# Moving the splitting of pass-2 weights and gated values from GpSimd to VectorE and ScalarE

## The chip, the cores and the metric

The kernel runs on one core of a Trainium2 chip. The metric is the device time of one execution, in microseconds (us). Five engines work in parallel, each with its own queue of instructions which it takes strictly in order: TensorE (PE in the profile, its weight loads PEld), VectorE (DVE), ScalarE (ACT), GpSimd (POOL) and SyncE (SP, which here issues the DMAs). An instruction that waits for a semaphore holds up all that stand behind it on the same engine.

## The reference

```
x = causal attention of 4 x 8 heads, 576 tokens, head size 64   -> x [2304, 512]
h = x @ w_in                       # w_in  [512, 2048]
g = h * clip(h + 3, 0, 6) / 6      # the gate
x2 = g @ w_out                     # w_out [2048, 512]
m = max(x2 @ w1, x2 @ w2, x2 @ w3) # each [512, 768]
out = m @ w_out2                   # [768, 512]
```

All inputs are float32 to the caller; the weights reach the chip as 64-bit floating-point words of the same values, so each weight tile is first decoded from integer bits to float32.

## The kernel before, in words

Nearly every matrix product is done as three matmuls on a split operand pair (`three`, L427): both factors are held as a high half (the value rounded to the matmul's float32r format) and a low half (the value minus its high half), and high x high, high x low and low x high are added up in one PSUM bank. So every operand has to be split once: one rounding copy (`rounded`, L326) and one subtraction (`minus`, L344) with two inputs in SBUF.

The work has four stages: attention (until about 345 us in the trace), the first hidden layer (`hidden1`, `gate`, `reduce1`), the second one (`hidden2`, products with combined weights and inputs) and the last product (`reduce2`). The first hidden layer runs in two passes. Pass 1 (z = 0) takes the first 6 of 16 blocks of 128 hidden channels, for all 8 units of 288 tokens, and lies partly under the attention. Pass 2 (z = 1) takes the other 10 blocks for all 8 units. For each unit and block PE makes 12 matmuls into a PSUM bank (tile ps_h); then `gate` runs four steps: ACT writes `u` (L955), DVE writes `g` (L959) and with that frees the PSUM bank, ACT rounds `g` into the high half of `gt` (L331, called gh here), and a subtraction writes the low half (L346, called gl). PE then uses `gt` for 12 matmuls of `reduce1` (tile ps_x), which go between those of later gates.

The 20 late weight blocks (10 of w_in, 10 of w_out) are decoded when attention is over, between about 366 and 463 us: a 512 KB DMA into `raw` (two buffers), a square on ACT (L385), four DVE instructions on 128x512 (L387, L393, L398, L403), and then the two halves of `w`: the rounding (L333, called wh) and the subtraction (L346, called wl). Six more blocks, of w_out2 (keys "o2"), go through the same code later. The `raw` buffer is free after L403, so the next load is issued then.

Which engine does a splitting step is looked up in the table `ON` (L226). Where an entry names two engines, the one that is free first in a planner takes it: the whole kernel is written by small threads which a simulated clock (`Flow`, L108) advances with assumed costs (`COST`, L316), and the instructions of each engine are put into the program in the order in which the planner dispatches them. So an entry in `ON` sets not only where an instruction runs but can also move later ones, on all engines.

Of the kernel before, what the change touches and what calls it, by code (L numbers as in the profile page):

```python
# [9 lines left out]
F32 = mybir.dt.float32  # L10
# [18 lines left out]
U1 = S // 2  # L29
# [3 lines left out]
NA = 6  # L33
# [170 lines left out]
def dve2(n):  # L204
    return 0.068 + n * 0.00104
# [6 lines left out]
def act2(n):  # L212
    return 0.051 + n / 1200.0
# [6 lines left out]
def pool2(n):  # L220
# [3 lines left out]
DMA = ("SP", 0.45)  # L224
POOL, ACT, DVE = ("POOL",), ("ACT",), ("DVE",)
ON = {  # L226
    "wh": DVE,
    "wl": POOL,
    ("qb", "h", True): ACT,
    ("qb", "h", False): POOL + ACT,  # L230
    ("qb", "l", True): POOL + DVE,
# [14 lines left out]
    "xh": ACT + DVE,  # L246
    "xl": POOL,
    "gh": ACT,
    "gl": POOL + DVE,
    "part": ACT,  # L250
}

# [2 lines left out]
def attn_moe_moe2(ctx, tc, q, k, v, s, w_in, w_out, w1, w2, w3, w_out2, out):  # L255
# [40 lines left out]
    def make(item, shape, dtype, name):  # L296
        pl, tag = item
        if pl is None:
            return views[tag]
        return pl.tile(shape, dtype, tag=tag, name=name, bufs=1)  # L300
# [10 lines left out]
    def round_to(dst, src):  # L311
        pool.tensor_scalar(
            out=dst, in0=src, scalar1=1.0, scalar2=1.0, op0=ALU.mult, op1=ALU.mult
        )
# [11 lines left out]
    def rounded(dst, src, n, engines):  # L326
        e = yield [(x, COST["copy"][x](n)) for x in engines]
        if e == "POOL":
            round_to(dst, src)
        elif e == "ACT":  # L330
            act.activation(dst, src, AF.Copy)  # L331
        else:
            vec.tensor_copy(dst, src)  # L333
# [10 lines left out]
    def minus(dst, a, b_, n, engines):  # L344
        e = yield [(x, COST["sub"][x](n)) for x in engines]
        (pool if e == "POOL" else vec).tensor_tensor(  # L346
            out=dst, in0=a, in1=b_, op=ALU.subtract
        )
# [21 lines left out]
    def weight(key):  # L370
        return ready.setdefault(key, event())

    def bits_in(src, out):
        r = yield RAW.get()
        raw = make(r, [P, 512], I64, "raw")
        yield DMA
        copy(raw, src)
        yield flow.landing(8 * P * 512)
        am = yield AM.get()
        m = make(am[1], [P, 512], F32, "dm")  # L380
        a = make(am[0], [P, 512], U32, "da") if out is None else out.bitcast(U32)
        bits = raw.bitcast(U32).rearrange("p (n t) -> p n t", t=2)
        lo, hi = bits[:, :, 0], bits[:, :, 1]
        yield "ACT", act1(512)
        act.activation(m, hi.bitcast(F32), AF.Square)  # L385
        yield "DVE", dve2(512)
        vec.scalar_tensor_tensor(  # L387
            out=m, in0=m, scalar=LEAST * LEAST, in1=hi.bitcast(F32),
            op0=ALU.is_ge, op1=ALU.mult,
        )  # L390
        top = m.bitcast(U32)
        yield "DVE", dve1(512)
        vec.tensor_scalar(  # L393
            out=a, in0=top, scalar1=3, scalar2=0x3FFFFFF8,
            op0=ALU.logical_shift_left, op1=ALU.bitwise_and,
        )
        yield "DVE", dve2(512)
        vec.scalar_tensor_tensor(  # L398
            out=a, in0=top, scalar=0xC0000000, in1=a,
            op0=ALU.bitwise_and, op1=ALU.bitwise_or,  # L400
        )
        yield "DVE", dve2(512)
        vec.scalar_tensor_tensor(  # L403
            out=a, in0=lo, scalar=29, in1=a,
            op0=ALU.logical_shift_right, op1=ALU.bitwise_or,
        )
        RAW.put(r)
        if out is not None:
            AM.put(am)
        return a.bitcast(F32), am  # L410

    def decode(src, store, key):
        item = yield store.get()
        wf, am = yield from bits_in(src, None)
        dst = make(item, [P, 2, 512], F32R, "w")
        yield from rounded(dst[:, 0, :], wf, 512, ON["wh"])
        yield from minus(dst[:, 1, :], wf, dst[:, 0, :].bitcast(F32), 512, ON["wl"])
        AM.put(am)
        weight(key).set((dst, item))

# [509 lines left out]
    def hidden1():  # L930
        for z in range(2):
            for u in range(NU):
                x, xi = yield x_ready[z, u]
                for f in range(z * NA, NA if z == 0 else NF):
                    w, wi = yield weight(("i", f))
                    gi = yield GT.get()
                    bank = yield M.get()
                    ps = make(bank, [P, U1], F32, "ps_h")
                    for kk in range(KD):
                        yield "PE", 3 * mm(U1), kk < KD - 1  # L940
                        three(
                            ps, w_slice(w, kk), (x[:, 0, kk, :], x[:, 1, kk, :]),
                            kk == 0, kk == KD - 1,
                        )
                    flow.start(flow.cur.prio, gate(z, u, f, ps, bank, gi))
                    if u == NU - 1:
                        (W if z == 0 else W2).put(wi)
                X.put(xi)
        x_over.set()

    def gate(z, u, f, ps, bank, gi):
        ui = yield UU.get()
        ut = make(ui, [P, U1], F32, "u")
        yield "ACT", act2(U1) + 0.093
        act.activation(ut, ps, AF.Relu, bias=half, scale=1.0 / 6.0)  # L955
        g2 = yield GG.get()
        g = make(g2, [P, U1], F32, "g")
        yield "DVE", dve2(U1)
        vec.scalar_tensor_tensor(  # L959
            out=g, in0=ut, scalar=1.0, in1=ps, op0=ALU.min, op1=ALU.mult  # L960
        )
        M.put(bank)
        UU.put(ui)
        t = make(gi, [P, 2, U1], F32R, "gt")
        yield from rounded(t[:, 0, :], g, U1, ON["gh"])
        yield from minus(t[:, 1, :], g, t[:, 0, :].bitcast(F32), U1, ON["gl"])
        GG.put(g2)
        gt_ready[z, u, f].set((t, gi))

# [100 lines left out]
    def out_weight(j):  # L1070
        yield from decode(w_out2[j], W, ("o2", j))
        w, item = weight(("o2", j)).value
        ev = yield from load(o2_d[j], w, 8 * P * 512)
        yield ev
        W.put(item)
        o2_stored[j].set()
# [307 lines left out]
    def main():  # L1384
# [15 lines left out]
        for f in range(NB):  # L1400
            flow.start(NS + f, decode(w_in[NA + f], W2, ("i", NA + f)))
        for f in range(NB):
            flow.start(NS + AFTER + f, decode(w_out[NA + f], W2, ("o", NA + f)))
# [130 lines left out]
```

## Time and profile before

| | |
|---|---|
| time, median of 3 runs | 982.18 us (979.78 to 984.79) |
| the profiled execution | 978.72 us |
| its span, first to last instruction | 976.9 us |
| PE busy | 931.7 us (95%) |
| PE weight loads busy | 870.5 us (89%) |
| VectorE busy | 701.5 us (72%) |
| ScalarE busy | 451.7 us (46%) |
| GpSimd busy | 390.0 us (40%) |

An engine's busy time says how long its instructions were running, waits for a shared resource inside an instruction included. The shares are averages over stages; rows of single stretches follow below. A matmul of 288 columns shows about 0.29 us, but consecutive ones start about 0.13 us apart.

### The profile page before, as it was taken

Reading aid. Unit: us, or ns where it says so; the run is one execution under the profiler, and the core shown is the slowest. Engines: PE = TensorE matmul, PEld = TensorE weight load, DVE = VectorE, ACT = ScalarE, POOL = GpSimd, SP = SyncE. Lnnn points to the kernel's source line nnn. Section 1 sums busy time; section 2 is a strip of 40 time slices with the busy share of each in tenths; the row PEclk is TensorE's granted clock in tenths of the full one; section 3 lists DMA queues with packets and bytes.
Section 4 is the critical chain, followed back from the end, with each engine's and each line's share of the span. In section 5 each row is a group of like instructions: output and inputs, shape, how many; then the busy total and the mean of one; then the engine's idle time right before and its main releaser. Section 6 shows DMA issues by size and latency. Waiting matters only on the chain.

```text
span 976.9 us, 19063 instructions
## 1 busy us (share of the span) xinstructions
PE 931.7 (95%) x6532; PEld 870.5 (89%) x6532; DVE 701.5 (72%) x1819; ACT 451.7 (46%) x1146; POOL 390.0 (40%) x430
## 2 busy tenths in 40 slices
PE   9988799999899999899999999999899999999998
PEld 5555589888889999899999999998899999999998
DVE  5899899878898729999548777449987676666300
ACT  3566488676776734343433334334433232333321
POOL 5578668555665324444324332226731000011000
PEclk7789799999999999999999999999899999999999
DMA  5689778695785345554545646401312120255522
GB/s 173 177 225 275 206 184 221 168 256 161 182 229 140 118 136 167 185 184 149 170 157 176 227 148 214 141 18 32 86 51 73 38 85 31 94 182 147 160 78 74
DMA packets 87482, 144.56 MB, mean 148 GB/s; under 512 B 9532, under 2 KB 58684, under 8 KB 87384
## 3 DMA queue, kind: packets, MB, share of 16 engines
q1 hardware_dynamic: 87384, 143.33, 50.4%
q8 instruction: 52, 0.85, 0.4%
q14 instruction: 46, 0.38, 0.1%
HBM read 82.79 MB, written 33.96 MB: 120 GB/s over the span
## 4 chain that ended last, share of the span: by engine, by line
PE 66%; DVE 14%; DMA 9%; issue 5%; POOL 2%; ACT 2%; SPq 2%; DVEq 0%; POOLq 0%; ACTq 0%
PE ps_j L430 6%; PE ps_j L431 6%; PE ps_j L429 6%; PE ps_s L762 6%; PE ps_x L429 4%; PE ps_h L429 4%; PE ps_h L430 4%; PE ps_x L431 4%; PE ps_h L431 4%; PE ps_x L430 4%; PE pt L826 3%; DMA kt<-kb 3%; PE px L867 3%; PE ps_o L430 3%; PE ps_o L431 3%
## 5 line engine op out<-in xcount | busy, mean ns | idle before, releaser
L429 PE MATMUL ps_x<-gt,w 128*128 128x288 f32 x512 | 153.8, 300 | 6.1 <-DVE g L959 5.5
L346 POOL TENSOR_TENSOR gt<-g,gt 128x288 fp32r<-128x288 f32 x100 | 87.8, 878 | 179.3 <-ACT gt L331 169.0
L429 PE MATMUL ps_h<-x,w 128*128 128x288 f32 x512 | 153.9, 301 | 0.3 <-DVE g L959 0.3
L431 PE MATMUL ps_x<-gt,w 128*128 128x288 f32 x512 | 152.2, 297 | 1.4 <-POOL w L346 1.4
L430 PE MATMUL ps_h<-x,w 128*128 128x288 f32 x512 | 151.7, 296 | 0.0
L430 PE MATMUL ps_x<-gt,w 128*128 128x288 f32 x512 | 151.3, 295 | 0.0
L431 PE MATMUL ps_h<-x,w 128*128 128x288 f32 x512 | 151.1, 295 | 0.0
L340 POOL TENSOR_SCALAR e<-e,tiny 128x256 f32<-128x256 f32 (+4 forms) x152 | 106.4, 706 | 92.2 <-DVE tiny L791 47.3
L430 PE MATMUL ps_j<-xf,wf 128*128 128x288 f32 x432 | 129.5, 300 | 3.1 <-POOL xf L346 2.7
L429 PE MATMUL ps_j<-xf,wf 128*128 128x288 f32 x432 | 128.7, 298 | 2.1 <-DVE xf L333 2.0
L431 PE MATMUL ps_j<-xf,wf 128*128 128x288 f32 x432 | 128.7, 298 | 0.0
L785 ACT ACTIVATE e<-e,tiny 64x576 f32<-64x576 f32 (+4 forms) x160 | 95.8, 599 | 41.4 <-DVE tiny L777 32.0
L331 ACT ACTIVATE gt<-g 128x288 fp32r<-128x288 f32 x128 | 56.4, 442 | 120.0 <-DVE g L959 119.1
L762 PE MATMUL ps_s<-kt,qt 66*128 66x256 f32 (+11 forms) x384 | 102.2, 362 | 8.4 <-DMA kt<-kb 5.5
L429 PEld LDWEIGHTS ps_x<-gt,w 128*128 128x128 f32 x512 | 97.1, 190 | 8.0 <-DVE g L959 6.6
L959 DVE SCALAR_TENSOR_TENSOR g<-u,ps_h 128x288 f32<-128x288 f32 x128 | 57.2, 447 | 58.3 <-ACT u L955 56.6
L431 PEld LDWEIGHTS ps_x<-gt,w 128*128 128x128 f32 x512 | 97.2, 190 | 1.9 <-POOL w L346 1.9
L429 PEld LDWEIGHTS ps_h<-x,w 128*128 128x128 f32 x512 | 96.9, 189 | 1.3 <-DVE g L959 0.5
L430 PEld LDWEIGHTS ps_x<-gt,w 128*128 128x128 f32 x512 | 97.3, 190 | 0.1
L430 PEld LDWEIGHTS ps_h<-x,w 128*128 128x128 f32 x512 | 96.9, 189 | 0.1
L431 PEld LDWEIGHTS ps_h<-x,w 128*128 128x128 f32 x512 | 96.8, 189 | 0.0
L955 ACT ACTIVATE u<-ps_h,half 128x288 f32<-128x288 f32 x128 | 63.5, 496 | 61.2 <-PE ps_h L431 60.6
(149 smaller groups left out, 2250.1 us busy)
## 6 DMA issues: line engine op xcount, KB each, us to landing
x<-x_d SPq DMA_DIRECT2D x64, 288.0 KB
kt<-kb SPq DMA_DIRECT2D x90, 144.0 KB
raw<-in_w_out_dram SPq DMA_DIRECT2D x22, 512.0 KB
x_d<-xs SPq DMA_DIRECT2D x16, 576.0 KB
raw<-in_w_dram SPq DMA_DIRECT2D x18, 512.0 KB
qt<-qb SPq DMA_DIRECT2D x30, 288.0 KB
raw<-in_w_in_dram SPq DMA_DIRECT2D x16, 512.0 KB
mh<-m_d SPq DMA_DIRECT2D x48, 144.0 KB
```

Source lines behind the costliest of these rows:

```text
L331: act.activation(dst, src, AF.Copy)
L340: (pool if e == "POOL" else vec).tensor_scalar(out=y, in0=y, scalar1=r, scalar2=1.0, op0=ALU.mult, op1=ALU.mult)
L346: (pool if e == "POOL" else vec).tensor_tensor(out=dst, in0=a, in1=b_, op=ALU.subtract)
L429: pe.matmul(ps, lhsT=wh, rhs=xh, start=first, stop=False, skip_group_check=again)
L430: pe.matmul(ps, lhsT=wh, rhs=xl, start=False, stop=False, skip_group_check=again)
L431: pe.matmul(ps, lhsT=wl, rhs=xh, start=False, stop=last, skip_group_check=again)
L762: pe.matmul(o, lhsT=lhs[:, qs], rhs=rhs[:, lo:hi], start=(x == 0), stop=(x == len(passes) - 1),)
L785: act.activation(e[:n, :w], e[:n, :w], AF.Exp, bias=m0, scale=-1.0, accum_out=r,)
L826: pe.transpose(pt[:, y, :], cut, ident[:n, :n])
L867: pe.matmul(px[:, z:n], lhsT=vhl[:, x, j].rearrange("p l d -> p (l d)"), rhs=src[:, hl, x, z:n], start=(x + hl == 0), stop=(last and hl == 1),
L955: act.activation(ut, ps, AF.Relu, bias=half, scale=1.0 / 6.0)
L959: vec.scalar_tensor_tensor(out=g, in0=ut, scalar=1.0, in1=ps, op0=ALU.min, op1=ALU.mult)
```

## The change

The table `ON` gets keys that tell the passes apart. For weights decoded late (blocks 6 to 15 and the "o2" blocks) wh is made by ACT instead of DVE, and wl by DVE instead of POOL. In pass 2, gl is made by DVE alone; before, POOL or DVE took it. Everything in pass 1 keeps its engines.

```
-    "wh": DVE,
-    "wl": POOL,
+    ("wh", False): DVE,
+    ("wh", True): ACT,
+    ("wl", False): POOL,
+    ("wl", True): DVE,
...
-    "gl": POOL + DVE,
+    ("gl", 0): POOL + DVE,
+    ("gl", 1): DVE,
...
-        yield from rounded(dst[:, 0, :], wf, 512, ON["wh"])
-        yield from minus(dst[:, 1, :], wf, dst[:, 0, :].bitcast(F32), 512, ON["wl"])
+        late = key[0] == "o2" or key[1] >= NA
+        yield from rounded(dst[:, 0, :], wf, 512, ON["wh", late])
+        yield from minus(dst[:, 1, :], wf, dst[:, 0, :].bitcast(F32), 512, ON["wl", late])
...
-        yield from minus(t[:, 1, :], g, t[:, 0, :].bitcast(F32), U1, ON["gl"])
+        yield from minus(t[:, 1, :], g, t[:, 0, :].bitcast(F32), U1, ON["gl", z])
```

What this moves on VectorE, at the start of the late decodes (`dm`, `da` are the decode's steps, `w` the split weight, `g` and `gt` the gate's tiles). Before:

```order
L403 SCALAR_TENSOR_TENSOR da<-raw,da 128x512
L959 SCALAR_TENSOR_TENSOR g<-u,ps_h 128x288
L333 CAST w<-da 128x512
L393 TENSOR_SCALAR da<-dm 128x512
L346 TENSOR_TENSOR gt<-g,gt 128x288
L398 SCALAR_TENSOR_TENSOR da<-dm,da 128x512
L403 SCALAR_TENSOR_TENSOR da<-raw,da 128x512
L959 SCALAR_TENSOR_TENSOR g<-u,ps_h 128x288
L333 CAST w<-da 128x512
L346 TENSOR_TENSOR gt<-g,gt 128x288
```

The same place on VectorE after the change (line numbers are up to four higher):

```order
L406 SCALAR_TENSOR_TENSOR da<-raw,da 128x512
L963 SCALAR_TENSOR_TENSOR g<-u,ps_h 128x288
L396 TENSOR_SCALAR da<-dm 128x512
L349 TENSOR_TENSOR w<-da,w 128x512
L401 SCALAR_TENSOR_TENSOR da<-dm,da 128x512
L406 SCALAR_TENSOR_TENSOR da<-raw,da 128x512
L963 SCALAR_TENSOR_TENSOR g<-u,ps_h 128x288
L349 TENSOR_TENSOR w<-da,w 128x512
```

Each cast of `w` has become a subtraction, one or two places later, and the two subtractions of `gt`, which belong to pass 1 here, have gone to GpSimd.

On GpSimd, from the end of attention on (`xs` is the last attention output, `xrT` belongs to the second hidden layer). Before:

```order
L346 TENSOR_TENSOR xs<-x_4538,xs 128x576
L346 TENSOR_TENSOR gt<-g,gt 128x288 x3
L346 TENSOR_TENSOR w<-da,w 128x512 x2
L346 TENSOR_TENSOR gt<-g,gt 128x288
L346 TENSOR_TENSOR w<-da,w 128x512
L346 TENSOR_TENSOR gt<-g,gt 128x288
```

The same place on GpSimd after the change:

```order
L349 TENSOR_TENSOR xs<-x_4538,xs 128x576
L349 TENSOR_TENSOR gt<-g,gt 128x288 x17
L1094 TENSOR_TENSOR xrT_7018<-xr_6926,xrT_6916 128x576
L1094 TENSOR_TENSOR xrT_6916<-xrT_6916,xr_6902 128x576
L1094 TENSOR_TENSOR xrT_7076<-xr_6940,xrT_7056 128x576
L349 TENSOR_TENSOR wf<-wr,wf 128x2x256
```

After the 17 subtractions that are left of pass 1, GpSimd has nothing to do for weights or gates; what follows is work for the second hidden layer. On ScalarE one rounding of `w` per late weight is added, between the gate's instructions:

```order
L959 ACTIVATE u<-ps_h,half 128x288
L334 ACTIVATE w<-da 128x512
L334 ACTIVATE gt<-g 128x288
L959 ACTIVATE u<-ps_h,half 128x288
L334 ACTIVATE w<-da 128x512
L334 ACTIVATE gt<-g 128x288
```

Before, `u` and the rounding of `gt` stand next to each other there. Over the whole program VectorE loses 26 casts of `w` and gains 26 subtractions of `w` and 60 of `gt`; GpSimd loses 26 and 60; ScalarE gains 26 roundings. Where the planner could choose, it now chooses otherwise in the second hidden layer's preparation: the 128x2x256 subtractions of `wf` go from 6 on VectorE and 3 on GpSimd to 1 and 8, and a few others change sides. The order of the matmuls on PE stays the same but for one group of three, which comes later.

## Rows read from the trace of the kernel before

**Rows 1.** Stretches from:to, length, busy PE, PEld, DVE, ACT, POOL; granted clock; DMA share; GB/s.

```profile
366.00:465.00 99.00, 92.38 (x677) 90.98 (x677) 94.64 (x138) 39.62 (x88) 45.65 (x37) 0.98 0.55 170
465.00:676.00 211.00, 209.75 (x1580) 208.79 (x1579) 135.95 (x242) 81.37 (x175) 73.12 (x77) 1.00 0.47 148
676.00:726.00 50.00, 43.28 (x291) 41.69 (x290) 48.95 (x91) 20.80 (x56) 34.18 (x36) 0.93 0.19 54
726.00:900.00 174.00, 174.00 (x1310) 174.00 (x1309) 118.30 (x281) 53.76 (x137) 15.52 (x15) 1.00 0.29 91
```

**Rows 2.** PE's waits, 366 to 465 us: total us, times, longest.

```profile
PE ps_x L429 <- DVE g L959: 5.2, 4, 2.7
PE ps_x L431 <- POOL w L346: 1.4, 2, 0.8
```

**Rows 3.** PE's waits, 676 to 726 us.

```profile
PE ps_j L430 <- POOL xf L346: 2.7, 2, 1.5
PE ps_j L429 <- DVE xf L333: 2.0, 1, 2.0
```

**Rows 4.** VectorE's groups, 366 to 465 us: busy us, mean ns, idle before.

```profile
L398 DVE SCALAR_TENSOR_TENSOR da<-dm,da 128x512 uint32<-128x512 uint32 x20 | 16.7, 836 | 0.6
L387 DVE SCALAR_TENSOR_TENSOR dm<-dm,raw 128x512 f32<-128x512 f32 x20 | 16.5, 825 | 4.6 <-ACT dm L385 4.5
L403 DVE SCALAR_TENSOR_TENSOR da<-raw,da 128x512 uint32<-128x512 uint32 x20 | 15.8, 791 | 0.4
L393 DVE TENSOR_SCALAR da<-dm 128x512 uint32<-128x512 uint32 x20 | 15.0, 749 | 0.5
L333 DVE CAST w<-da 128x512 fp32r<-128x512 f32 x20 | 12.8, 642 | 0.4
L959 DVE SCALAR_TENSOR_TENSOR g<-u,ps_h 128x288 f32<-128x288 f32 x28 | 12.5, 445 | 0.9 <-ACT u L955 0.9
L346 DVE TENSOR_TENSOR gt<-g,gt 128x288 fp32r<-128x288 f32 x10 | 12.4, 1239 | 1.0 <-ACT gt L331 1.0
```

**Rows 5.** GpSimd's groups in the same stretch.

```profile
L346 POOL TENSOR_TENSOR w<-da,w 128x512 fp32r<-128x512 f32 x20 | 30.2, 1510 | 29.8 <-DVE w L333 29.5 <-PE ps_x L431 0.4
L346 POOL TENSOR_TENSOR gt<-g,gt 128x288 fp32r<-128x288 f32 x17 | 16.1, 946 | 26.2 <-ACT gt L331 26.2
```

**Rows 6.** VectorE in order of time, while GpSimd idles: start us, us.

```profile
391.44 0.44 DVE L346 TENSOR_TENSOR gt<-g,gt 128x288 fp32r<-128x288 f32 x1
...
392.26 0.69 DVE L398 SCALAR_TENSOR_TENSOR da<-dm,da 128x512 uint32<-128x512 uint32 x1
```

**Rows 7.** VectorE in order of time, around PE's longest wait.

```profile
411.50 1.64 DVE L403 SCALAR_TENSOR_TENSOR da<-raw,da 128x512 uint32<-128x512 uint32 x1
413.06 0.44 DVE L959 SCALAR_TENSOR_TENSOR g<-u,ps_h 128x288 f32<-128x288 f32 x1
413.43 0.42 DVE L333 CAST w<-da 128x512 fp32r<-128x512 f32 x1
414.01 1.51 DVE L346 TENSOR_TENSOR gt<-g,gt 128x288 fp32r<-128x288 f32 x1 [0.17 <-ACT gt L331]
```

**Rows 8.** GpSimd in order of time, the same moments.

```profile
410.95 1.65 POOL L346 TENSOR_TENSOR w<-da,w 128x512 fp32r<-128x512 f32 x1 [0.37 <-DVE w L333]
413.92 1.28 POOL L346 TENSOR_TENSOR w<-da,w 128x512 fp32r<-128x512 f32 x1 [1.33 <-DVE w L333]
```

**Rows 9.** ScalarE rounding 128x512 elsewhere: group of 366 to 700 us.

```profile
L331 ACT ACTIVATE wf<-wr 128x512 fp32r<-128x512 f32 x6 | 3.7, 619 | 0.0
```

**Rows 10.** Issue of one late weight's load, by the DMA queue.

```profile
437.88 0.33 SPq L306 DMA_DIRECT2D raw<-in_w_out_dram  x1
```

**Rows 11.** ScalarE's first step on that load.

```profile
441.85 0.69 ACT L385 ACTIVATE dm<-raw 128x512 f32<-128x512 f32 x1 [2.29 <-DMA raw<-in_w_out_dram]
```

**Rows 12.** GpSimd while PE waits for the second layer's first inputs.

```profile
679.67 2.81 POOL L346 TENSOR_TENSOR xf<-xrT,xf 128x288 fp32r<-128x288 f32 x3
```

**Rows 13.** VectorE at the same moment.

```profile
681.75 0.89 DVE L333 CAST xf<-xr 128x288 fp32r<-128x288 f32 x1
```

## The prediction

> **What bounds the kernel now.** I read the page's busy shares first: PE 95%, VectorE 72%, GpSimd 40%. As averages over stages they say little, so the next view is the table of stretches [rows 1]; its columns are start and end, length, busy us of PE, PEld, DVE, ACT and POOL with counts, granted clock, DMA share and GB/s. The reader is to see three kinds of stretch. From 726 to 900 us PE is busy for all 174 us, and from 465 to 676 us it idles for 1.25 us of 211: there nothing but PE's own work counts. From 366 to 465 us, where the 20 late weights are decoded, PE idles for 99 - 92.38 = 6.6 us and VectorE is busy for 94.64 of 99 us. From 676 to 726 us, where the second layer's inputs are prepared, PE idles for 50 - 43.28 = 6.7 us and VectorE is busy for 48.95 of 50 us. The granted clock adds a second loss. It is at its lower level (1.2 GHz) for some microseconds behind PE's idle time: a mean of 0.98 over 99 us is 2.0 us of full-speed work lost, and 0.93 over 50 us is 3.5 us. So the first of these stretches loses 8.6 us and the second 10.2 us.
>
> Then PE's waits. In the first stretch 5.2 us are waits for `g` on VectorE and 1.4 us for the low half of a weight on GpSimd [rows 2]. PE needs `g` because that instruction frees the PSUM bank that ps_x takes next. In the later stretch PE waits mostly for the low half of an input on GpSimd and for a cast on VectorE [rows 3].
>
> Why is VectorE so full from 366 us on? Its groups there [rows 4] and GpSimd's [rows 5] are to be read against single instructions. While GpSimd idles, the subtraction of `gt` takes 0.44 us and a decode step 0.69 us [rows 6]. The same forms took 1.51 us and 1.64 us, and the decode's last step ended only when GpSimd's subtraction ended [rows 7, 8]: 410.95 + 1.65 = 412.60 on GpSimd, 413.14 on VectorE. `g`, which reads one operand from PSUM, takes 0.44 us on average and never stretches, but it stood behind that step, and PE waited 2.7 us for it. So a good part of VectorE's busy time is time in which it is held up by GpSimd.
>
> The Trainium skill (SBUF — State Buffer, "Who interferes with whom") says that VectorE and GpSimd share one pair of ports, that the pair is an exclusive lock held for the whole instruction, and that a VectorE instruction with two SBUF inputs or in a two-port mode is fully blocked while a GpSimd instruction reads SBUF. The rows above agree: 1.64 against 0.69 us.
>
> **The change part by part.** All sums are made for the profiled execution, 978.72 us, which lies 3.5 us below the median of the runs shown (982.18 us).
>
> How much VectorE is held up between 366 and 465 us: mean minus free duration, times the count [rows 4, 6, 7]. L398, L387 and L403: 20 x (0.146 + 0.135 + 0.101) = 7.6 us. L393, taken at the cast's 0.42 us (both have one input, the same shape and similar means): 20 x 0.33 = 6.6 us. The cast: 20 x 0.22 = 4.4 us. The 10 subtractions of `gt`: 10 x 0.80 = 8.0 us. Together 26.6 us, so VectorE's own work is 94.6 - 26.6 = 68 us.
>
> What the change removes: 20 casts of 0.42 us, 8.4 us. What it adds: 20 subtractions of `w`. The trace shows no free one of just this kind that I rest on; between 0.42 us (cast, one input) and 0.84 us (L398, stretched) I take 0.69 us, the free L398, which has the same shape and two SBUF inputs [rows 6]: 13.8 us. Of the 28 gates in the stretch about 15 still belong to pass 1 (95 of the 128 gates start after 366 us, so 33 of pass 1's 48 are done), and these subtractions go to GpSimd by the new order; the other 13 go to VectorE, 3 more than now: 1.3 us. VectorE's work becomes 68 - 8.4 + 13.8 + 1.3 = 75 us.
>
> What GpSimd keeps there is 15 x 0.95 = 14 us in place of 30.2 + 16.1 = 46.3 us [rows 5]. If it holds VectorE up in the same proportion, 26.6 x 14 / 46.3 = 8 us remain, all before about 420 us. So VectorE has 83 us of work in some 92 us, where now it has 95 in 99; past 420 us nothing holds it up. `g` then comes close to its place in the plan, and I let 1.5 of the 5.2 us of waits for it stand. The 1.4 us for the weight on GpSimd go with GpSimd, but the next in line is the decode itself, since the last weights of the first pass-2 unit come just in time. A load took 3.97 us from issue to ScalarE's first step, which waited 2.29 us for it [rows 10, 11]; then come 0.69 us there and about 3.5 us on VectorE (L387, the previous weight's subtraction, one gate, L393, L398, L403, and a subtraction of `gt`, at free durations that overlap by some 0.08 us each), and 0.4 us to the next issue. That is 8.6 us for a buffer, 4.3 us for a weight with two buffers: 20 weights end at 366 + 86 = 452 us, against 463 us now, and PE without its losses would ask for the last one at about 463 - 8.6 = 454 us. I keep 1 us of waiting for this, with 0 to 6 us as its ends. If PE waits less, the clock's loss of 2.0 us goes too, or partly: 1.0 us stays. Gain of the stretch: 8.6 - 1.5 - 1 - 1 = 5, with -3 to 8.6 us as ends.
>
> The 26 roundings on ScalarE cost 0.62 us each by another tile of that shape [rows 9], 12.4 us in the stretch, on top of 39.62 us busy of 99 [rows 1]. I cost them at nothing; ScalarE's idle time is the cover. The price if it is gone: each stands ahead of the next `u` or rounding of `gt` and waits for VectorE's L403, so a late decode step now delays a gate by way of ScalarE too, up to one step's 0.7 us for a gate.
>
> From 465 to 676 us all of 1.25 us idle is to be had; the longer VectorE queue takes 60 x 0.44 us more there and in the neighbouring stretches, minus what is no longer held up, beside 75 us of idle time. I take a gain of 1 us.
>
> From 676 to 726 us the change works only through the plan. GpSimd is 34.18 us busy there, and in the worst moment three of its subtractions in a row [rows 12] stretch VectorE's cast to 0.89 us [rows 13], for which PE waits. The last gates' subtractions leave GpSimd, but the planner fills it with wide subtractions of `wf` and takes work off VectorE for that. Both signs are possible; I take 0, with 5 us to either side (half of what is lost there).
>
> Sum: 978.7 - 5 - 1 = 972.7 us, on the scale of the median 982.2 - 6 = 976 us. As PE is busy without a gap from 726 us on, what is won earlier reaches the end.
>
> **The rivals.**
>
> A: the queue clears wholly, and the second layer's preparation profits as well (its critical subtractions on an emptier VectorE). For it: 26.6 us of held-up time, and fewer VectorE instructions between the last two gates in the new order. Against it: GpSimd gets more wide instructions just there. 8.6 + 1.25 + 4 = 14 us, 968 us.
>
> B: the decode's loads take over. If a weight still needs 4.7 us (now 97 us for 20), PE waits for weights in place of `g`, and only 2 us are won: 980 us. For it: ScalarE waits for loads already now [rows 11]. Against it: 4.3 us by the sum above.
>
> C: the busy time is real work and not a lock. Then VectorE, at 95 us of 99, gets 20 x 0.84 - 12.8 = 4 us for `w` and 3 x 1.24 = 4 us for `gt`, 103 us in all, and PE waits for the whole excess beyond what it does now: 8 us longer, 990 us. It decides from the point at which VectorE's work passes the stretch's length. Against it: 0.44 and 1.51 us for one form [rows 6, 7].
>
> The Trainium skill (Perfetto Trace Analysis, "Optimizing Scalar/DVE Operations") speaks for C's direction: where VectorE is saturated, work may be offloaded from it to ScalarE or even GpSimd, though between GpSimd and VectorE, which share a port, that "might not help". This change goes the other way, so by the first half of the rule it would be slower and by the second about the same. The trace so far bears out the second half, since what GpSimd does costs VectorE time.
>
> D: the second layer's preparation gets worse by 5 us and cancels the gain, 981 to 985 us.
>
> **How the numbers follow.** About 0.5% (4.9 us) is what a measurement of this kernel can tell from no change, so faster means below 977.3 us and slower above 987.1 us. My forecast, 976 us with a range of its own from 972 to 980, has 0.50; A 0.19; B 0.13; C 0.07; D 0.11. Faster: 0.50 x 0.75 + 0.19, and 0.03 of B's, is 0.6. Slower: C and a small part of D, 0.09. The rest, 0.31, is no change. The range goes from 966 us (A with a little more) to 984 us (most of D) and leaves out C and the far ends, under 2 in 10.
>
> **What would show it.** Right: between 366 and 455 us VectorE's 128x512 steps at 0.69 and 0.42 us past the last pass-1 gates, VectorE below 90% busy there, PE's waits for `g` under 2 us, the late decodes done by about 455 us. Wrong: the same durations still stretched with GpSimd idle (C), waits of PE for `w` behind loads (B), or more than 10 us lost around the start of the second layer (D).

## The result, and the profile after

The changed kernel took 971.97 us (median of 6 runs, 968.39 to 974.36) against 981.88 us for the kernel before (6 runs). The ratio is 0.9902, with a 95% interval of 0.9878 to 0.9926: faster by about 1%. The profiled execution took 971.03 us. From its page:

```profile
span 969.2 us, 18930 instructions
...
PE 926.9 (96%) x6532; PEld 867.4 (89%) x6532; DVE 691.5 (71%) x1880; ACT 467.5 (48%) x1172; POOL 300.2 (31%) x343
```

The span was 976.9 us before. The stretches of the trace (start:end, length, busy us of PE, PEld, DVE, ACT, POOL with counts, granted clock, DMA share, GB/s), to be read against [rows 1]; the borders of the later two are 11 us earlier, since the work arrives earlier:

```profile
366.00:465.00 99.00, 97.84 (x735) 96.94 (x734) 85.02 (x151) 53.98 (x115) 14.94 (x15) 1.00 0.59 183
465.00:665.00 200.00, 200.00 (x1515) 200.00 (x1514) 138.03 (x282) 82.01 (x173) 17.69 (x17) 1.00 0.46 150
665.00:740.00 75.00, 66.25 (x461) 64.53 (x460) 64.21 (x135) 28.82 (x76) 30.09 (x31) 0.93 0.18 53
```

Three things are to be seen. While the late weights are decoded (366 to 465 us) PE idles for 1.2 us where it idled for 6.6 us, and the clock stays at its upper level. In the rest of pass 2 PE does not idle at all. At the start of the second layer (665 to 740 us) PE idles for 8.75 us, and a clock of 0.93 over 75 us costs 5.2 us more: 14 us lost. The same length of the kernel before lost 6.7 us by idling and 3.75 us by the clock:

```profile
676.00:751.00 75.00, 68.28 (x479) 66.69 (x478) 66.07 (x133) 29.46 (x78) 34.18 (x36) 0.95 0.22 64
```

PE's waits between 366 and 465 us (total us, times, longest), which answer to [rows 2]:

```profile
PE ps_h L433 <- DVE g L963: 0.6, 1, 0.6
PE ps_x L433 <- DVE g L963: 0.4, 1, 0.4
```

The 5.2 us of waits for `g` have become 1.0 us, and the 1.4 us for a weight's low half are gone. VectorE's groups in that stretch (busy us, mean ns | idle before), which answer to [rows 4]; line numbers are three or four higher than before:

```profile
L401 DVE SCALAR_TENSOR_TENSOR da<-dm,da 128x512 uint32<-128x512 uint32 x20 | 15.9, 793 | 0.4
L406 DVE SCALAR_TENSOR_TENSOR da<-raw,da 128x512 uint32<-128x512 uint32 x20 | 15.3, 766 | 0.3
L390 DVE SCALAR_TENSOR_TENSOR dm<-dm,raw 128x512 f32<-128x512 f32 x20 | 15.2, 759 | 10.1 <-ACT dm L388 10.1
L963 DVE SCALAR_TENSOR_TENSOR g<-u,ps_h 128x288 f32<-128x288 f32 x31 | 13.9, 447 | 1.2 <-ACT u L959 1.2
L349 DVE TENSOR_TENSOR w<-da,w 128x512 fp32r<-128x512 f32 x20 | 13.7, 687 | 3.0 <-ACT w L334 3.0
L396 DVE TENSOR_SCALAR da<-dm 128x512 uint32<-128x512 uint32 x20 | 10.1, 503 | 0.2
L349 DVE TENSOR_TENSOR gt<-g,gt 128x288 fp32r<-128x288 f32 x16 | 7.3, 455 | 1.5 <-ACT gt L334 1.5
```

The subtraction of `gt` has come down from 1239 to 455 ns on average, L393's successor L396 from 749 to 503 ns, and the new subtraction of `w` takes 687 ns. Past GpSimd's last subtraction of pass 1 (it ended at 417.4 us) the decode's steps have their free lengths, 423 to 689 ns on average from 424 to 457 us; the shortest of them:

```profile
L396 DVE TENSOR_SCALAR da<-dm 128x512 uint32<-128x512 uint32 x7 | 3.0, 423 | 0.0
```

In the whole stretch VectorE makes 151 instructions in 85.02 us where it made 138 in 94.64 us. GpSimd's and ScalarE's groups there:

```profile
L349 POOL TENSOR_TENSOR gt<-g,gt 128x288 fp32r<-128x288 f32 x15 | 14.9, 996 | 39.5 <-ACT gt L334 37.1 <-PE ps_x L435 2.4
```

```profile
L388 ACT ACTIVATE dm<-raw 128x512 f32<-128x512 f32 x20 | 13.5, 673 | 13.8 <-DMA raw<-in_w_out_dram 7.6 <-DMA raw<-in_w_in_dram 6.1
L334 ACT ACTIVATE w<-da 128x512 fp32r<-128x512 f32 x20 | 12.6, 630 | 9.9 <-DVE da L406 9.7
```

GpSimd has kept the 15 subtractions of pass 1's last gates [rows 5], and ScalarE's roundings take 630 ns.

What was lost again stands in PE's waits between 465 and 740 us, to be read against [rows 3]:

```profile
PE ps_j L434 <- POOL xf L349: 3.9, 1, 3.9
PE ps_j L434 <- DVE xf L349: 2.6, 3, 1.7
PE ps_j L433 <- DVE mm L1241: 2.0, 1, 2.0
```

The longest, 3.9 us, waited for a subtraction of `xf` on GpSimd. In order of time on GpSimd (start us, us), and the matmul that waited:

```profile
681.33 0.98 POOL L1094 TENSOR_TENSOR ws<-wr,ws 128x256 f32<-128x256 f32 x1
682.67 0.72 POOL L1094 TENSOR_TENSOR wr<-wr 128x256 f32<-128x256 f32 x1 [0.36 <-DVE ws L1094]
683.36 0.94 POOL L349 TENSOR_TENSOR wg<-wr,wg 128x256 fp32r<-128x256 f32 x1
684.26 0.84 POOL L349 TENSOR_TENSOR xf<-xr,xf 128x288 fp32r<-128x288 f32 x1
```

```profile
685.15 0.61 PE L434 MATMUL ps_j<-xf,wf 128*128 128x288 f32 x1 [3.94 <-POOL xf L349]
```

The subtraction ran from 684.26 us, as soon as GpSimd was through with `ws`, `wr` and `wg`, three steps for weight forms that stood ahead of it.

Executions differ by some microseconds in the attention stage, which none of these kernels changes on purpose, so single traces are compared from the 33rd gate on (the 33rd `g`, behind attention). The table gives by how much each profiled execution gains (-) or loses (+) against the profiled execution of before between four marks: the starts of the 33rd, 65th and 128th `g` and of the last reading of a second-layer bank by VectorE. The first part is the decoding of late weights, the second the rest of pass 2, the third the second layer's start. A single mark may be off by about 1 us, since a `g` moves a little against PE.

| kernel | late weights | rest of pass 2 | second layer's start | ratio of times (95%) |
|---|---|---|---|---|
| the change | -8.0 | -2.8 | +3.4 | 0.9902 (0.9878 to 0.9926) |
| e1 GpSimd repeats wl | +5.9 | -2.8 | +2.5 | 1.0054 (1.0022 to 1.0086) |
| e2 weights alone | -6.1 | -0.1 | 0.0 | 0.9932 (0.9899 to 0.9965) |
| e3 gates alone | -0.5 | -2.8 | +1.9 | 0.9969 (0.9938 to 0.9999) |
| e4 cast back on VectorE | -8.1 | -2.2 | +5.4 | 0.9908 (0.9877 to 0.9938) |
| e5 xf on VectorE | -8.0 | +0.5 | -1.3 | 0.9917 (0.9887 to 0.9946) |
| e6 all splits on VectorE | -7.6 | -3.3 | +1.2 | 0.9861 (0.9826 to 0.9895) |
| e7 GpSimd silent | -8.5 | -4.3 | +1.1 | 0.9913 (0.9880 to 0.9946) |
| e9 repeat, result unused | +7.6 | -2.8 | +3.9 | 1.0089 (1.0058 to 1.0121) |
| e10 e6 and pass 1's gates | -12.6 | -3.3 | +1.3 | 0.9863 (0.9815 to 0.9910) |

In e5 the last gate itself is late, so its second and third part are to be added. e8 is left out: its attention is not over at the 33rd gate. In e4 and e10 the first column flatters: the planner has put some of PE's matmuls on `ps_x` behind the third mark. Between the first two marks there are 398 with the change and 384 in e4 (the count in brackets behind the first busy time), and 380 in e10:

```profile
361.15:466.83 105.68, 73.50 (x398) 59.41 (x397) 1.73 (x4) 5.16 (x14) 1.00 0.61 190
```

```profile
361.94:467.56 105.62, 70.85 (x384) 57.16 (x383) 1.81 (x4) 5.29 (x14) 1.00 0.57 181
```

At about 0.13 us from one matmul to the next, that moves some 2 us from the third column to the first in these two rows.

### The profile page after: what moved, and what is told of

Same layout as the page of the kernel before. It is cut to its first block, busy times and chain, and to the rows that moved or that the text cites. A ratio compares the mean times of both kernels' runs of the same rounds, so it can differ in the third digit from the quotient of the medians.

```text
span 969.2 us, 18930 instructions
## 1 busy us (share of the span) xinstructions
PE 926.9 (96%) x6532; PEld 867.4 (89%) x6532; DVE 691.5 (71%) x1880; ACT 467.5 (48%) x1172; POOL 300.2 (31%) x343
## 4 chain that ended last, share of the span: by engine, by line
PE 71%; DMA 11%; DVE 10%; issue 3%; SPq 2%; ACT 1%; POOL 1%; DVEq 0%; POOLq 0%; ACTq 0%
PE ps_j L434 7%; PE ps_j L435 7%; PE ps_j L433 7%; PE ps_x L435 5%; PE ps_h L433 5%; PE ps_x L433 5%; PE ps_h L434 5%; PE ps_h L435 5%; PE ps_s L766 5%; PE ps_x L434 5%; DMA kt<-kb 4%; PE pt L830 3%; PE px L871 3%; PE ps_o L434 3%; PE ps_o L435 3%
## 5 line engine op out<-in xcount | busy, mean ns | idle before, releaser
L433 PEld LDWEIGHTS ps_x<-gt,w 128*128 128x128 f32 x512 | 96.1, 188 | 1.2 <-DVE g L963 0.6
L435 PEld LDWEIGHTS ps_x<-gt,w 128*128 128x128 f32 x512 | 96.2, 188 | 0.4 <-DVE w L349 0.3
L434 PEld LDWEIGHTS ps_x<-gt,w 128*128 128x128 f32 x512 | 96.2, 188 | 0.1
L781 DVE CUSTOM_DVE_ANT_0 e<-ps_s,above 64x288 f32<-64x288 f32 (+4 forms) x160 | 75.1, 473 | 27.5 <-PE ps_s L766 26.4
L434 PEld LDWEIGHTS ps_j<-xf,wf 128*128 128x128 f32 x432 | 82.6, 191 | 7.5 <-POOL xf L349 4.1
```

The lines of the kernel that those rows point to most:

```text
L433: pe.matmul(ps, lhsT=wh, rhs=xh, start=first, stop=False, skip_group_check=again)
L434: pe.matmul(ps, lhsT=wh, rhs=xl, start=False, stop=False, skip_group_check=again)
L435: pe.matmul(ps, lhsT=wl, rhs=xh, start=False, stop=last, skip_group_check=again)
L781: vec.tensor_tensor_reduce(out=e[:n, lo:hi], in0=ps[:n, 0:hi - lo], in1=above[:n, shift + lo:shift + hi], scale=-0.125, scalar=m0, op0=ALU ...
```

## The experiments

**Is it GpSimd's work that slows VectorE, or the new order?** Theory L: GpSimd's instructions hold VectorE up, and the gain is their absence. Rival P: the gain comes from the new order and from the cast's move to ScalarE. e1 gives GpSimd the late weights' subtraction once more, behind VectorE's, outside the planner's count, so that the other four engines keep the changed kernel's order:

```
         yield from minus(dst[:, 1, :], wf, dst[:, 0, :].bitcast(F32), 512, ON["wl", late])
+        if late:
+            pool.tensor_tensor(
+                out=dst[:, 1, :], in0=wf, in1=dst[:, 0, :].bitcast(F32), op=ALU.subtract
+            )
```

> The changed kernel, and GpSimd repeats each late weight's low-half subtraction once more behind VectorE's (26 instructions of 128x512, same values); the order of the instructions on the four other engines is that of the changed kernel. Theory L (GpSimd's instructions hold VectorE up): between 366 and 465 us VectorE's 128x512 steps are stretched again, mean of L393's successor over 0.6 us instead of some 0.45, VectorE over 95% busy there, PE waits for g again, and the time goes back by 5 to 8 us, to 977 to 980 us. Rival P (the gain came from the new order and from the cast's move to ScalarE, not from GpSimd's silence): VectorE's durations stay short, PE waits at most for the repeated subtraction of the last weights, 972 to 974 us.

Measured: 988.59 us (10 runs), ratio 1.0054, slower than the kernel before by 0.5% and than the changed kernel by 1.0054 / 0.9902 = 1.5%. Its late-weight stretch (columns as above):

```profile
366.00:465.00 99.00, 89.86 (x653) 87.54 (x652) 91.62 (x131) 48.33 (x104) 42.00 (x33) 0.98 0.56 178
```

PE's waits in that stretch (total us, times, longest):

```profile
PE ps_x L437 <- DVE g L967: 4.4, 3, 2.5
PE ps_x L439 <- POOL w L423: 3.0, 3, 1.2
```

The waits for `g` are back, but 3.0 us of waits are PE's for the repeated result itself, so e1 alone does not prove L. The time also lies 8.6 us above L's 977 to 980 us. Of L's signs, L393's successor is at 672 ns (over 0.6 us was expected), but VectorE is busy for 93% of the stretch and not for over 95%. e9 removes PE's wait for the repeat: it writes into the weight's spent decode tile, for which PE never waits (the first line stands behind L403's successor, the others behind VectorE's subtraction).

```
+        spent[am] = m
...
+        if late:
+            pool.tensor_tensor(
+                out=spent[am], in0=wf, in1=dst[:, 0, :].bitcast(F32), op=ALU.subtract
+            )
```

> As e1, but GpSimd's repeated subtraction writes into the weight's spent decode tile, so that PE never waits for it; only ScalarE's square of the weight after next can. The order on the four other engines is that of the changed kernel. Theory L: PE's 5 us of waits for GpSimd in e1 vanish, VectorE's decode steps stay stretched (mean of 0.85 us and more for the three-operand steps against 0.77 us), PE waits for g: 976 to 983 us. Rival P: once nobody waits for GpSimd's result, the changed kernel's time comes back, 971 to 973 us.

Measured: 988.86 us (10 runs), ratio 1.0089 (1.0058 to 1.0121). The stretch, PE's waits in it, and three of VectorE's groups:

```profile
366.00:465.00 99.00, 89.24 (x641) 87.50 (x640) 89.83 (x125) 47.02 (x101) 43.25 (x34) 0.96 0.53 169
```

```profile
PE ps_x L440 <- DVE g L970: 8.1, 4, 3.1
PE ps_x L442 <- DVE w L349: 1.5, 1, 1.5
```

```profile
L349 DVE TENSOR_TENSOR w<-da,w 128x512 fp32r<-128x512 f32 x18 | 23.3, 1294 | 2.4 <-ACT w L334 2.4
L392 DVE SCALAR_TENSOR_TENSOR dm<-dm,raw 128x512 f32<-128x512 f32 x18 | 16.9, 937 | 5.9 <-ACT dm L390 5.8
...
L398 DVE TENSOR_SCALAR da<-dm 128x512 uint32<-128x512 uint32 x18 | 13.0, 722 | 0.2
```

And one moment, first VectorE, then GpSimd (start us, us):

```profile
407.49 1.77 DVE L349 TENSOR_TENSOR w<-da,w 128x512 fp32r<-128x512 f32 x1
```

```profile
407.40 1.31 POOL L426 TENSOR_TENSOR dm<-da,w 128x512 f32<-128x512 f32 x1 [1.36 <-ACT w L334]
```

GpSimd's useless repeat ran from 407.40 to 408.71 us, and VectorE's subtraction, which takes 0.69 us alone, began at 407.49 us and took 1.77 us. PE waits 8.1 us for `g` behind such steps. The instructions and their order on VectorE, ScalarE, PE and SP are those of the changed kernel, and neither VectorE nor ScalarE shows a wait for GpSimd in the stretch: the time is lost inside VectorE's instructions. So P falls. The time went up more than L expected (983 us at most). The trace has what may explain it: VectorE now makes the subtraction itself and is held up by GpSimd's in just that instruction (1294 ns on average), which the kernel before did not have, and the granted clock was 0.96 against 0.98 before. Only 18 of the 20 decodes end in the stretch. How much of the miss each of these makes was not measured.

**Which part of the change brings what?** e2 keeps only the weights' part, e3 only the gates' part:

```
e2:
-    ("gl", 1): DVE,
+    ("gl", 1): POOL + DVE,
e3:
-    ("wh", True): ACT,
+    ("wh", True): DVE,
-    ("wl", True): DVE,
+    ("wl", True): POOL,
```

> Only the weights' part of the change: late high halves by ScalarE, late low halves by VectorE; the low half of gated values stays with GpSimd or VectorE. Theory L: the 30 us of weight subtractions on GpSimd were the longer and denser blocks in the first stretch, so most of its 8 us is won here, and the 2 us won later (465 to 676 us) are not: about 975 us. Rival P: the weights' part alone adds 5 us of VectorE work to a full VectorE, so it wins nothing, 980 to 985 us.

> Only the gates' part of the change: in pass 2 the low half of gated values is made by VectorE alone; late weights stay as before (cast on VectorE, subtraction on GpSimd). Theory L: GpSimd still blocks VectorE for 30 us while weights are decoded, so the first stretch wins 0 to 3 us; later, where only gates are left on GpSimd, the 2 us are won: 977 to 980 us. Rival P (the order of the gates matters): the whole gain of 8 to 10 us, 972 us.

Measured: 974.68 us for e2 and 977.76 us for e3 (10 runs each). Both as L expected. In the table the weights' part gains 6.1 us while weights are decoded and nothing elsewhere; the gates' part gains 0.5 us there, 2.8 us in the rest of pass 2, and loses 1.9 us at the second layer's start. In e3 GpSimd is still busy for 40 us of the first stretch and PE idle for 6.4 us:

```profile
366.00:465.00 99.00, 92.61 (x681) 91.46 (x680) 93.27 (x146) 39.65 (x88) 40.13 (x29) 0.98 0.56 177
```

**Does the cast's move to ScalarE count?** e4 undoes that alone:

```
-    ("wh", True): ACT,
+    ("wh", True): DVE,
```

> The changed kernel, but the late weights' high halves are made by VectorE again (26 casts of 0.42 us), low halves and gates as in the change. Theory L with the load as I summed it: VectorE has 20 x 0.34 = 7 us more between 366 and 455 us, on about 83 us of some 90, so it is full again, 2 to 4 us slower than the changed kernel, 974 to 976 us. Rival (GpSimd's silence is all that matters and ScalarE's part is idle): 972 us, no difference.

Measured: 973.63 us (7 runs), ratio 0.9908 against 0.9902. This lies between the two expectations, and the intervals overlap almost wholly. The trace of the stretch, where VectorE is busy for 92.16 us:

```profile
366.00:465.00 99.00, 96.14 (x720) 95.00 (x719) 92.16 (x169) 42.70 (x95) 14.48 (x15) 1.00 0.56 177
```

PE idles for 2.9 us here and for 1.2 us with the change, and some 2 us of the -8.1 us in the table are matmuls put off. So by the trace the cast's move is worth some 2 us of the stretch's 8; the times are too coarse to show it. A VectorE nearly full with GpSimd mostly silent hurt PE far less than a VectorE nearly full and held up (94.64 us busy before, PE idle for 6.6 us).

**Why does the second layer's start lose 3.4 us?** My theory T after the trace: the one subtraction of `xf` on GpSimd. e5 gives those to VectorE:

```
-    FORM = (DVE + POOL, DVE)
+    FORM = (DVE, DVE)
```

> The changed kernel, and the low halves of the second layer's first inputs (xf of the first pair of units) are made by VectorE alone; GpSimd keeps its share of the combined weights. Theory T (the 3.4 us that the second layer's start gave back are PE's 3.9 us wait for one xf subtraction, which stood on GpSimd behind four of its weight steps): that wait goes, 2 to 4 us faster than the changed kernel, 968 to 970 us. Rival V (VectorE is full there anyway, over 95% busy, so what leaves GpSimd comes back as VectorE's lateness): 972 us, within 1 us.

Measured: 971.78 us (6 runs), ratio 0.9917: no gain, as the rival said. The 3.9 us wait for GpSimd is gone, and in its place PE waits for VectorE's subtractions of `xf`:

```profile
PE ps_j L434 <- DVE xf L349: 5.6, 4, 3.1
```

T as I had put it falls: the wait moved. e6 takes every split's subtraction there from GpSimd, e7 the sums and differences as well:

```
e6, beside e5's edit, in split_form:
-        yield from minus(lo, src, hi.bitcast(F32), n, DVE + POOL)
+        yield from minus(lo, src, hi.bitcast(F32), n, DVE)
e7, beside e6's, in combined:
-        e = yield [("DVE", dve2(n)), ("POOL", pool2(n))]
+        e = yield [("DVE", dve2(n))]
```

> As before it, and all subtractions of splits in the second layer's preparation (xf, wf, wg) go to VectorE; GpSimd keeps sums and differences (ws, wr, xrT). Theory T with the hold-up: 16 of GpSimd's subtractions less, each of which held VectorE for about half its length, against some 16 more of 0.4 to 0.7 us on VectorE: no worse than e5, 967 to 970 us. Rival V: VectorE gets 8 us more work in 60 us in which it is full, PE waits longer, 974 to 980 us.

> All of the second layer's preparation on VectorE and ScalarE; from the end of the pass-1 gates on GpSimd does nothing until the last stage. Theory T with the hold-up: VectorE's instructions all run at their free durations; 42 us of GpSimd work become some 23 us on VectorE, of which some 19 us come back as hold-up saved: 968 to 972 us. Rival V: 976 us or more, since VectorE's work between 645 and 725 us exceeds the time.

Measured: e6 965.80 us (6 runs), ratio 0.9861 (0.9826 to 0.9895), below even T's 967 to 970 us, so V falls; e7 970.18 us (7 runs), ratio 0.9913, within T's range. That e6 beats the change (0.9878 to 0.9926) is likely and not shown, since the ends of the two intervals overlap. In e6 the second layer's start:

```profile
665.00:740.00 75.00, 69.36 (x483) 68.17 (x482) 63.66 (x149) 28.89 (x78) 19.30 (x17) 0.93 0.21 65
```

GpSimd is busy for 19.30 us there in place of 30.09, VectorE for 63.66 in place of 64.21 although it makes 149 instructions in place of 135, and PE idles for 5.6 us in place of 8.75. So what GpSimd did not do cost VectorE nothing net. In e7 nothing holds VectorE up, but PE stood 5.9 us for one copy out of PSUM on ScalarE:

```profile
PE ps_j L433 <- ACT mm L1237: 5.9, 1, 5.9
```

ScalarE in order of time shows why:

```profile
688.39 0.42 ACT L334 ACTIVATE wf<-wr 128x256 fp32r<-128x256 f32 x1 [0.59 <-DVE wr L1094]
691.44 0.42 ACT L334 ACTIVATE wf<-ws 128x256 fp32r<-128x256 f32 x1 [2.62 <-DVE ws L1094]
...
692.59 0.39 ACT L1237 ACTIVATE mm<-ps_j 128x288 f32<-128x288 f32 x1
```

The copy at 692.59 us stood behind a rounding of `wf` at 691.44 us that waited 2.6 us for VectorE's `ws`, after three such waits. With all sums on VectorE the chain of weight forms runs through VectorE and ScalarE by turns, and PE's copies stand behind it in ScalarE's queue. So hold-up is one part of what the start of the second layer loses, and the order in which VectorE's and ScalarE's queues wait for each other is another.

**Can the planner be told?** e8 counts GpSimd's two-input instructions at twice their length in the planner.

```
-        "sub": {"POOL": pool2, "DVE": dve2},
+        "sub": {"POOL": lambda n: 2 * pool2(n), "DVE": dve2},
...
-        e = yield [("DVE", dve2(n)), ("POOL", pool2(n))]
+        e = yield [("DVE", dve2(n)), ("POOL", 2 * pool2(n))]
```

> The changed kernel, and the planner counts GpSimd's two-input instructions at twice their length, so that it gives GpSimd fewer of them (about 51 in place of 80 after attention, fewer in pass 1's gates too) and expects their results later. Theory T: GpSimd's lateness comes from the hold-up which the plan does not know; with it counted, the second layer's start loses 2 to 4 us less and pass 1 a little less too: 967 to 970 us. Rival V: 972 us or slower.

Measured: 991.91 us (6 runs), ratio 1.0130 (1.0101 to 1.0158). T missed by 22 us. V's range (972 us or slower) holds the time, which by itself says little, since the edit reaches the attention stage too. From 300 us on, in e8:

```profile
300.00:366.00 66.00, 63.62 (x469) 59.59 (x469) 56.29 (x224) 48.91 (x137) 35.53 (x47) 1.00 0.63 165
366.00:465.00 99.00, 93.47 (x681) 91.16 (x681) 65.00 (x126) 49.18 (x107) 16.86 (x19) 0.98 0.52 165
```

From 300 to 366 us VectorE is busy for 56.29 us, against 39.82 us in the kernel before, and the first late weight is split only at 406.9 us, against 371.3 us. So the time decides nothing about T. The trace has PE losing less from the 128th gate on: 4.0 us by idling in e8, 7.8 us with the change and 4.8 us before. But some 45 matmuls on `ps_x` that other kernels make earlier lie there in e8 and can cover waits, so T is not shown by that either.

**What if GpSimd is silent while late weights are decoded?** e10 is e6, and pass 1's gates go to VectorE as well once attention is over:

```
-        yield from minus(t[:, 1, :], g, t[:, 0, :].bitcast(F32), U1, ON["gl", z])
+        late = z == 1 or attention_done.time is not None
+        yield from minus(t[:, 1, :], g, t[:, 0, :].bitcast(F32), U1, ON["gl", int(late)])
```

> e6, and the low halves of pass 1's gates go to VectorE too once attention is over, so that GpSimd is silent while the late weights are decoded. Theory L: the last hold-up there (some 6 us on VectorE, 1 us of PE's waits) goes: 0 to 1.5 us faster than e6, 964 to 966 us. Rival V: VectorE gets 14 x 0.37 = 5 us more and PE's waits stay, 966 us or slower.

Measured: 966.13 us (6 runs), ratio 0.9863 (0.9815 to 0.9910): as fast as e6, which is the rival's number. Its trace is the clean case of the whole study, GpSimd silent while weights are decoded:

```profile
366.00:465.00 99.00, 99.00 (x752) 99.00 (x751) 83.77 (x167) 55.84 (x116) 0.00 (x0) 1.00 0.58 187
```

```profile
L349 DVE TENSOR_TENSOR gt<-g,gt 128x288 fp32r<-128x288 f32 x31 | 14.0, 452 | 0.5 <-ACT gt L334 0.4
L390 DVE SCALAR_TENSOR_TENSOR dm<-dm,raw 128x512 f32<-128x512 f32 x20 | 13.8, 690 | 9.7 <-ACT dm L388 9.6
...
L349 DVE TENSOR_TENSOR w<-da,w 128x512 fp32r<-128x512 f32 x20 | 13.7, 686 | 1.5 <-ACT w L334 1.4
...
L396 DVE TENSOR_SCALAR da<-dm 128x512 uint32<-128x512 uint32 x20 | 8.4, 421 | 0.0
```

PE idles for nothing at all, and every group of VectorE has its free length on average: 452, 690, 686 and 421 ns against 1239, 825 and 749 ns [rows 4] for the three that stood there before. The times show nothing of the -12.6 us in the table against e6's -7.6 us. Some 2 us of it are matmuls put off. For the rest, e10's three columns add up to -14.6 us, near what its ratio gives (-13.4 us), while e6's add up to -9.7 us and its ratio gives -13.6 us: the odd one is e6's single trace. Why is open.

## Why the prediction was right, point by point

**What bounds the kernel.** Right: the waits for `g` behind held-up VectorE steps. e9 shows the hold-up itself, with order and instructions unchanged, and e10 its absence. One reading was inexact: the held decode step did not end when GpSimd's subtraction ended but 0.54 us later (413.14 and 412.60 us), and in e9's pair VectorE's end, 409.26 us, lies 0.55 us behind GpSimd's, 408.71 us. So in both pairs most of the 0.69 us came only after GpSimd's end.

**The free length of the new subtraction.** Taken at 0.69 us by the free L398; 687 ns measured, and 686 ns in e10. L393 was taken at the cast's 0.42 us, on a thin argument (means of 749 and 642 ns); it is 421 ns in e10. ScalarE's rounding: 0.62 us taken, 0.63 us measured.

**The gain while weights are decoded.** Mis-sized: 5 us forecast, 8.0 us measured in the trace, of which PE's idle time makes 5.4 us (6.6 to 1.2) and the clock 2.0 us. Of what I let stand, the waits for `g` were 1.0 us (1.5 taken), the waits of PE's matmuls for weights none (1 taken), the clock's loss none (1 taken). The last late weight was ready at 455.8 us on VectorE, later than my 452 us and still early enough. I expected 8 us of hold-up to remain; by the groups above, with 0.69, 0.42 and 0.44 us as free lengths, it is 20 x (0.10 + 0.08 + 0.07 + 0.08) = 6.6 us.

**ScalarE at nothing.** Borne out: no wait of PE in the stretch names ScalarE, and e4, which takes the roundings off it again, is not faster.

**The rest of pass 2.** 1 us forecast, 2.8 us in the trace; e3 shows that it is the gates' part. Between the marks PE idles for 3.1 us before and 1.0 us after, so 2.1 us of it are idle time; the forecast's 1.25 us stopped at 676 us, and the mark lies at 682.6 us. The remaining 0.7 us are within what a mark may be off.

**The second layer's start.** 0 forecast with 5 us to either side; 3.4 us lost. The reason given, that the planner fills the emptied GpSimd with wide subtractions, is what the order shows and e6 makes good in part by taking them away (1.2 us lost in place of 3.4). That one subtraction was to blame, as I thought next, was refuted by e5.

**The sum.** 6 us forecast, 7.7 us by the spans of the profiled executions, 9.9 us by the medians. The two differ because the profiled execution of before lies 3.2 us below its median and that of after 0.9 us. That the three terms came out near the forecast is in part luck: the first two were too small by 4.8 us together, and the third, put at 0, took 3.4 us back.

**The rivals.** C, busy time as real work, would have been slower; e10 has more VectorE instructions in that stretch (167) than before (138) in less time (83.77 us). B did not come: ScalarE waited 13.8 us for loads of raw weights (12.5 us before), and no matmul of the stretch waited for a weight (one weight load did, for 0.3 us). D came in part, 3.4 of its 5 us, and did not cancel the gain. A's whole clearing is seen only in e10.

The Trainium skill's page Perfetto Trace Analysis ("Optimizing Scalar/DVE Operations") says that work may be moved from a saturated VectorE even to GpSimd, and that because of the shared port it might not help. Here its caution decides: with VectorE at 96% of the stretch, taking work back from GpSimd was faster by 8 us. The rule in the Trainium skill's page SBUF — State Buffer ("Who interferes with whom"), one holds and the other blocks for the whole instruction, agrees with e9's 1.77 us against 0.69 us.

## What to carry to other kernels

When VectorE looks full, compare the mean length of each of its groups with the shortest one of the same form, and see what GpSimd does in the long ones: busy time that is waiting inside an instruction goes away with the other engine's work, even if VectorE has to take that work over. Look for the instruction that PE waits for (here `g`, never stretched itself) and price what stands ahead of it on its queue. And where a planner chooses engines, an emptied engine can be filled elsewhere, as GpSimd was here with subtractions of `wf`: follow what it is given there, since the place may be critical.

## What was not expected of the hardware

An instruction of GpSimd whose result nobody needs is not free, though GpSimd has idle time for it. In e9, 26 of them at about 1.6 us, 41 us together, made the kernel 1.9% slower than the same program without them (1.0089 / 0.9902), some 18 us. By the table 15.6 us of that lie in the decoding of late weights (+7.6 against -8.0 us).

`g`, with one operand in PSUM and one in SBUF, took 445 to 450 ns in every kernel here, with GpSimd busy for 43 us of the stretch or for none; the forms with one or two SBUF operands and an SBUF result were those that stretched.

Profiled executions of these kernels start their 33rd gate up to 7 us apart (2.2 us before that of the kernel before in e5, 5.0 us after it in e2), though the changes begin later; a single span would have ranked e2 behind e4 by 3 us where the medians differ by 1 us.
